# First-batch keys less their maximum on TensorE, float32 attention products for two batches, and a replanned order

## The chip, the core and the metric

The kernel runs on one core of one Trainium2 chip. The metric is the device time of one execution in microseconds (us), as the median of several runs. An order of instructions is written out by a planner in the kernel itself, so an edit of one operation, or of one of the planner's prices, may move any other instruction on its engine.

## The reference, cut to what matters

Linear attention over four batches of eight heads (576 rows of 64), then two feed-forward layers over all 2304 rows:

```python
q_s = exp(q - max(q, axis=-1)); q_s = q_s / (sum(q_s, axis=-1) + 1e-9)
k_s = exp(k - max(k, axis=2));  k_s = k_s / (sum(k_s, axis=2) + 1e-9)
kv  = einsum('bhsd,bhse->bhde', k_s, v)
x   = einsum('bhsd,bhde->bhse', q_s, kv)   # then [2304, 512]
h = x @ w_in1;  x2 = (h * sigmoid(1.702 * h)) @ w_out1
h = x2 @ w_in2; out = (h * tanh(softplus(h))) @ w_out2
```

Shapes: w_in is 512 x 2048, w_out 2048 x 512, everything float32.

## The kernel before

Rows go in six blocks of 384 (NB). A batch of 576 rows is one and a half blocks, so blocks 1 and 4 straddle two batches. Per block, `attention(blk)` makes the transposed input `xt` of the first layer: a high part rounded to float32r and the low part that is left (`hi_lo`: ACT copies, DVE subtracts). Every large product is the sum of three float32r products, high by high, high by low and low by high (`SPLIT`).

A *unit* is one batch and one pair of heads (four units to a batch). `k_load` and `v_load` fetch it: k as one DMA whose rows are 1536 B long in both memories, v as two DMAs of 256 B pieces, because the tile `vt` leaves two columns of ones after each 64 columns (they give the sum of the exponentials). `k_max` forms the maximum of k over the rows: a strided `reduce_max` on DVE over six chunks (L444), a transpose on TensorE (L454), a second `reduce_max` (L456), and a transpose that spreads the result over partitions (L461). `k_kv` copies that to SBUF on ACT (L468), subtracts it from k on DVE or GpSimd (through the helper `either`, L321), exponentiates on ACT (L471), multiplies with v in float32 on TensorE (L477, twelve products, two records each), and divides by the sum: ACT writes the high part of `kv` (L498), DVE the low part (L505). The first batch has a PSUM bank (`acc`) for each unit; later ones share the bank `at[0]`.

For q, `q_soft` takes the softmax, `q_turn` transposes (L578) and splits the result into high and low (`hi_lo`, L565 on ACT and L570 on DVE, tile named g in the trace because `qT` is a part of g2), and `x_part` multiplies with `kv` in three float32r products (L596) and splits again into `xt`.

`weight` brings a 512 KB chunk of a weight matrix and reforms it: two scalings on ACT (L338), three DVE steps (L377, L384, L389), a high part copied by ACT (L329) and a low part subtracted on DVE (L321). Each layer has 32 chunks. The first layer's 12 matmuls for one of its 16 columns of h are `gemm_in` (L666), followed by `gelu` (L679, L684), `gelu_split` (L329, L321) and 12 matmuls of `gemm_out` (L707). The second layer is L666 into `hp` and L838. These matmuls are called the spine here.

`Plan` holds all of these operations with their engines, costs and dependences. `best()` places them by urgency, forward and backward, six times, and keeps the order whose modelled end is earliest. `either`, `copy` and `scaled` leave the engine to it. Before the first spine matmul it fills TensorE's gaps with transposes of the identity (`idle`, L873) and models the clock by the columns that went through (`clocked`). `attention(t + 1)` is handed in while block t runs; attention(0) comes first of all. All DMAs are issued on SP's queue in the planned order. Of the DVE and GpSimd operations some are marked as a pair that may not overlap (`from_pair`).

Of the kernel before, what the change touches and what calls it, by code (L numbers as in the profile page):

```python
# [19 lines left out]
class Plan:  # L20
# [18 lines left out]

    def op(self, ways, reads, writes):  # L40


        i = len(self.ops)
        before = {self.last_write.get(key) for key in [*reads, *writes]}
        for key in writes:
            before.update(self.readers.get(key, ()))
        for key in reads:
            self.readers.setdefault(key, []).append(i)
        for key in writes:
            self.last_write[key] = i  # L50
            self.readers[key] = []
        self.ops.append((ways, sorted(before - {None, i})))
# [22 lines left out]
    def order(self, links, urgency, ways=None):  # L75
# [33 lines left out]

        def clocked(t, begin, cost):  # L110
# [23 lines left out]
        while any(queues.values()):  # L134
# [16 lines left out]
            if e == PE and not ways:  # L151
                idle, cost = clocked(f, begin, cost)
                started = started or i == self.first
# [56 lines left out]
def tile_attention_moe_moe(  # L210
# [35 lines left out]
    NLATE = 3  # L246
    NRAW = 4
    ND = 3
    SPLIT = ((0, 0), (0, 1), (1, 0))
# [4 lines left out]

    ident = const.tile([P, P], F32, name="ident")
    W = [const.tile([P, 2, 1024], F32R, name=f"W{i}") for i in range(NFC - NLATE)]
    xt = [const.tile([P, NCC, 2, NB], F32R, name=f"xt{i}") for i in range(2)]
# [20 lines left out]
    kv = [ap.tile([P, 2, P], F32R, name=f"kv{i}") for i in range(NHP)]  # L278
    pmt = [ap.tile([KP, P], F32, name=f"pmt{i}") for i in range(NHP)]
    mcol = ap.tile([P, NHP], F32, name="mcol")  # L280
    rs = ap.tile([P, NHP], F32, name="rs")
    qs = ap.tile([P, 2, 12], F32, name="qs")
# [4 lines left out]
    kt += [sp.tile([KP, 2, KC, D], F32, name=f"kt{i}") for i in range(2, NHP)]  # L287
    vt += [sp.tile([KP, 2, KC, D + 2], F32, name=f"vt{i}") for i in range(1, NHP)]
    qr = [sp.tile([P, 4, NCT, D], F32, name=f"qr{i}") for i in range(2)]

    nc.scalar.preload_act_table_set("exp_and_others")
    make_identity(nc, ident)
    for t in vt:
        nc.gpsimd.memset(t[:, :, :, D : D + 2], 1.0)
# [11 lines left out]

    def pe(ns, reads, writes, fn):
        plan.op([(PE, ns, fn, False)], reads, writes)
# [41 lines left out]
    for i in range(NHP):  # L350
        plan.op([(POOL, 350.0, lambda i=i: nc.gpsimd.memset(f32(kv[i]), 0.0), False)], [], [("kv", i)])


# [70 lines left out]
    def v_load(u):  # L424
        b, hp = divmod(u, NHP)
        key = ("vt", v_tile(u))
        for j in range(2):
            dma(
# [7 lines left out]

    def k_max(u, ps1, ps2, key1, key2):
        kk = ("kt", k_tile(u))
        m = mcol[:, u % NHP : u % NHP + 1]
        dve(  # L440
            1310,
            [kk],
            [("pm", u % NHP)],
            lambda: nc.vector.reduce_max(  # L444
                out=pmt[u % NHP].rearrange("p (j d) -> p j d", j=2),
                in_=kt[k_tile(u)].rearrange("p j c d -> p j d c"),
                axis=AX.X,
            ),
        )
        pe(  # L450
            110,
            [("pm", u % NHP)],
            [key1],
            lambda: nc.tensor.transpose(ps1[:, 0:KP], pmt[u % NHP], ident[0:KP, 0:KP]),  # L454
        )
        dve(96, [key1], [("mc", u % NHP)], lambda: nc.vector.reduce_max(out=m, in_=ps1[:, 0:KP], axis=AX.X))  # L456
        pe(
            110,
            [("mc", u % NHP)],
            [key2],  # L460
            lambda: nc.tensor.transpose(ps2[0:KP, :], m.to_broadcast([P, KP]), ident),  # L461
        )

    def k_kv(u, ps2, ps3, key2, key3):
        kk = ("kt", k_tile(u))
        t, bc = kt[k_tile(u)], pmt[u % NHP]
        pk = ("pm", u % NHP)
        act(128, [key2], [pk], lambda: nc.scalar.activation(out=bc, in_=ps2[0:KP, :], func=AF.Copy), psum=True)  # L468
        m = bc.rearrange("p (j o d) -> p j o d", j=2, o=1).to_broadcast([KP, 2, KC, D])
        either(768, ALU.subtract, lambda: t, lambda: t, lambda: m, [kk, pk], [kk])  # L470
        act(768, [kk], [kk], lambda: nc.scalar.activation(out=t, in_=t, func=AF.Exp))  # L471

# [11 lines left out]

        pe(1375, [kk] + [("vt", v_tile(u), j) for j in range(2)], [key3], mm)

        o = kv[u % NHP]
        r = rs[:, u % NHP : u % NHP + 1]
        rk = ("rs", u % NHP)
        dve(1, [key3], [rk], lambda: nc.vector.tensor_scalar_add(r, ps3[:, D : D + 1], 1e-9))  # L490
        dve(1, [rk], [rk], lambda: nc.vector.reciprocal(r, r))
        for j in range(2):
            s = slice(j * D, (j + 1) * D)
            act(
                140,
                [key3, rk, ("kv", u % NHP)],
                [("kv", u % NHP, 0, j)],
                lambda s=s: nc.scalar.activation(out=o[s, 0, s], in_=ps3[s, 0:D], func=AF.Copy, scale=r[s, :]),  # L498
                psum=True,
            )  # L500
            dve(
                120,
                [key3, rk, ("kv", u % NHP, 0, j)],
                [("kv", u % NHP, 1, j)],
                lambda s=s: nc.vector.scalar_tensor_tensor(  # L505
                    out=o[s, 1, s],
                    in0=ps3[s, 0:D],
                    scalar=r[s, :],
                    in1=f32(o[s, 0, s]),
                    op0=ALU.mult,  # L510
                    op1=ALU.subtract,
                ),
            )
# [59 lines left out]
    def q_turn(blk, hp, ps, key):  # L573
        keys = [("qt", j, d) for j in (2 * (hp % 2), 2 * (hp % 2) + 1) for d in (0, 192)]

        def turn():
# [7 lines left out]
        pe(330, keys, [key], turn)  # L584
        t = qT[hp % 2]
        hi_lo(
            NB, lambda: t[:, 0, :], lambda: t[:, 1, :], lambda: ps[:, 0:NB], [key], ("qT", hp % 2, 0), ("qT", hp % 2, 1)
# [5 lines left out]
    def x_part(blk, hp, ps, key, r):  # L593
        def mm():
            for n, (a, b) in enumerate(SPLIT):
# [6 lines left out]
                )  # L602

        kvk = [("kv", hp, a, j) for a in range(2) for j in range(2)]
        n = NB if r is None else NB // 2
        i = 0 if r is None else r[0] // 64
        pe(521 if r is None else 340, kvk + [("qT", hp % 2, 0), ("qT", hp % 2, 1)], [key], mm)
        x = xt[blk % 2]
# [13 lines left out]
    def attention(blk):  # L622
# [3 lines left out]
        b = last[0]  # L626
        if blk == 0:
            kps = lambda hp: [(acc[hp][:, i * P : (i + 1) * P], ("acc", hp)) for i in range(3)]
        else:
            kps = lambda hp: [(at[0][:, i * P : (i + 1) * P], ("at", 0)) for i in range(3)]  # L630
        xps = lambda i: (at[1], ("at", 1)) if fresh and blk else (at[i % 2], ("at", i % 2))
        us = [b * NHP + hp for hp in range(NHP)] if fresh else []

        def unit(hp):
            u = us[hp]
            p = kps(hp)
            k_load(u)
            v_load(u)
            k_max(u, p[0][0], p[1][0], p[0][1], p[1][1])
            k_kv(u, p[1][0], p[2][0], p[1][1], p[2][1])  # L640

# [141 lines left out]
    def hb_keys(n):  # L783
        return [("h", 0), ("h", 1)] if (n + 1) % 2 == 0 else [("at", 0), ("at", 1)]

# [86 lines left out]
    def idle():  # L872
# [9 lines left out]
        + [("kt", i) for i in range(2, NHP)]  # L882
        + [("vt", i, j) for i in range(1, NHP) for j in range(2)]
        + [("qr", i) for i in range(2)],
    )
# [8 lines left out]
    for n in range(NS):  # L894
# [14 lines left out]
        if n == NS - NFC:  # L909
# [6 lines left out]
                + [("qt", j, d) for j in range(4) for d in (0, 192)]  # L916
                + [("kv", hp, a, j) for hp in range(NHP) for a in range(2) for j in range(2)]
                + [("pm", i) for i in range(NHP)]
                + [(s, i) for s in ("mc", "rs") for i in range(NHP)]
# [56 lines left out]
```

## Time and profile before

| what | us |
|---|---|
| median of 3 runs | 912.94 (912.01 to 913.74) |
| profiled execution, its own time | 910.09 |
| span of the profiled execution | 908.3 |
| TensorE matmul busy | 879.6 |
| VectorE (DVE) busy | 418.0 |
| ScalarE (ACT) busy | 364.1 |

The busy shares are means over stages with different limits, so the stages have to be read one by one: the slices of the page tell where an engine is full, the table by stretches tells how full, and the waits tell who was late there. "PE" is TensorE's matmul row, "PEld" its weight loads. Matmul ends are modelled and overlap, so the distance from the start of one group to the start of the next is a better measure of their rate than the busy time.

### The profile page before, as it was taken

How to read it: one execution, taken by the hardware profiler on the slowest of the kernel's cores; microseconds unless marked ns; L12 is line 12 of the kernel's file. 1: busy time of each engine (PE TensorE's matmuls, PEld its weight loads, DVE VectorE, ACT ScalarE, POOL GpSimd, SP SyncE). 2: the span in 40 equal slices, each digit the busy share in tenths (PEclk: the TensorE clock that was granted, in tenths of full speed). 3: DMA queues.
4: the chain of work that ended last, by engine and by line, in shares of the span. 5: the costliest groups of instructions: out<-in, count | busy, mean ns of one | idle time of the engine just before them, and what ended most of it. 6: DMA issues, size and time to landing. Idle time of an engine off the chain costs nothing.

```text
span 908.3 us, 12391 instructions
## 1 busy us (share of the span) xinstructions
PE 879.6 (97%) x5030; PEld 822.6 (91%) x5030; DVE 418.0 (46%) x758; ACT 364.1 (40%) x654; POOL 8.6 (1%) x18
## 2 busy tenths in 40 slices
PE   8897889999999999999999999999999999999998
PEld 7775669999998999999999999899999998998997
DVE  8999999255368247424899941110111011111100
ACT  4787674233245235323678841222222212212221
POOL 0001000000000000000000000000000000000000
PEclk9999999999999999999999999999999999999999
DMA  9665655002023112200245501001001001000000
GB/s 251 157 204 164 185 153 172 24 18 88 1 70 85 57 44 57 79 1 10 70 140 186 173 13 70 35 1 70 35 1 70 35 1 70 35 1 1 35 1 35
DMA packets 66616, 65.80 MB, mean 72 GB/s; under 512 B 37120, under 2 KB 57600, under 8 KB 66048
## 3 DMA queue, kind: packets, MB, share of 16 engines
q1 hardware_dynamic: 66560, 65.03, 23.7%
q8 instruction: 39, 0.64, 0.3%
q14 instruction: 17, 0.14, 0.1%
HBM read 54.00 MB, written 11.01 MB: 72 GB/s over the span
## 4 chain that ended last, share of the span: by engine, by line
PE 82%; DVE 8%; DMA 5%; ACT 2%; SPq 2%; issue 1%; DVEq 0%; ACTq 0%
PE hp L666 22%; PE acc L838 22%; PE acc L707 18%; PE h L666 17%; DMA raw<-in_moe_w_out_dram 2%; DMA raw<-in_moe_w_in_dram 2%; SPq L312 2%; PE at L477 1%; DVE dec L384 1%; DVE dec L389 1%; DVE pmt L444 1%; PE at L596 1%; DVE W L321 1%; PE at L578 1%; DMA qt<-in_q_dram 1%
## 5 line engine op out<-in xcount | busy, mean ns | idle before, releaser
L666 PE MATMUL h<-xt,W 128*128 128x384 f32 x1152 | 226.5, 340 | 9.7 <-DVE gt L684 4.8
L707 PE MATMUL acc<-g,W 128*128 128x384 f32 x1152 | 222.0, 338 | 1.8 <-DVE W L321 1.6
L666 PEld LDWEIGHTS h<-xt,W 128*128 128x128 f32 x1152 | 201.1, 189 | 16.4 <-DVE W L321 4.6
L666 PE MATMUL hp<-xt,W 128*128 128x384 f32 x1152 | 208.4, 335 | 0.0
L838 PE MATMUL acc<-W,g 128*128 128x512 f32 x864 | 206.1, 392 | 0.0
L666 PEld LDWEIGHTS hp<-xt,W 128*128 128x128 f32 x1152 | 201.9, 188 | 3.7
L707 PEld LDWEIGHTS acc<-g,W 128*128 128x128 f32 x1152 | 200.0, 188 | 4.1 <-DVE W L321 2.7
L838 PEld LDWEIGHTS acc<-W,g 128*128 128x128 f32 x864 | 161.6, 188 | 32.7
L321 DVE TENSOR_TENSOR g<-gt,g 128x384 fp32r<-128x384 f32 (+1 forms) x110 | 67.2, 611 | 173.1 <-ACT g L329 173.0
L321 DVE TENSOR_TENSOR g<-tb,g 128x768 fp32r<-128x768 f32 x32 | 30.6, 957 | 210.8 <-ACT g L329 210.8
L815 ACT ACTIVATE tb<-hp 128x768 f32<-128x768 f32 x32 | 26.0, 813 | 177.1 <-PE hp L666 177.1
L329 ACT ACTIVATE g<-gt 128x384 fp32r<-128x384 f32 (+1 forms) x112 | 63.7, 569 | 73.9 <-PE acc L707 68.3
L679 ACT ACTIVATE gt<-h 128x384 f32<-128x384 f32 x96 | 46.7, 488 | 89.5 <-PE h L666 89.1
L684 DVE SCALAR_TENSOR_TENSOR gt<-gt,h 128x384 f32<-128x384 f32 x96 | 52.6, 548 | 60.7 <-ACT gt L679 60.5
L815 ACT ACTIVATE gt<-hp 128x768 f32<-128x768 f32 x16 | 13.0, 812 | 96.3 <-PE hp L666 96.3
L338 ACT ACTIVATE dec<-raw 128x512 f32<-128x512 f32 x63 | 42.3, 675 | 18.5 <-DVE W L321 9.6
L338 ACT ACTIVATE raw<-raw 128x512 int32<-128x512 uint32 x63 | 42.5, 677 | 9.0 <-DMA raw<-in_moe_w_in_dram 5.1
L384 DVE SCALAR_TENSOR_TENSOR dec<-raw,dec 128x512 int32<-128x512 int32 x64 | 44.4, 694 | 0.3
L321 DVE TENSOR_TENSOR W<-dec,W 128x512 fp32r<-128x512 f32 x64 | 43.6, 681 | 0.6
L389 DVE CUSTOM_DVE_ANT_0 dec<-raw,dec 128x1024 uint16<-128x1024 uint16 x64 | 43.5, 683 | 0.2
L329 ACT ACTIVATE W<-dec 128x512 fp32r<-128x512 f32 x64 | 40.2, 629 | 8.0 <-DVE dec L389 8.0
L377 DVE TENSOR_SCALAR dec<-dec 128x512 int32<-128x512 int32 x64 | 27.7, 433 | 1.9 <-ACT dec L338 1.8
(65 smaller groups left out, 414.9 us busy)
## 6 DMA issues: line engine op xcount, KB each, us to landing
raw<-in_moe_w_in_dram SPq DMA_DIRECT2D x32, 512.0 KB, 3.8
raw<-in_moe_w_out_dram SPq DMA_DIRECT2D x32, 512.0 KB, 3.7
x2d<-xt SPq DMA_DIRECT2D x16, 384.0 KB, 3.2
xt<-x2d SPq DMA_DIRECT2D x4, 1536.0 KB, 6.3
kt<-in_k_dram SPq DMA_DIRECT2D x16, 288.0 KB, 4.5
vt<-in_v_dram SPq DMA_DIRECT2D x32, 144.0 KB, 3.7
out_dram<-dec SPq DMA_DIRECT2D x18, 256.0 KB, 2.1
qt<-in_q_dram SPq DMA_DIRECT2D x24, 96.0 KB, 2.8
```

The costliest lines, as they stand in the source:

```text
L321: return lambda: engine.tensor_tensor(out=out(), in0=in0(), in1=in1(), op=op)
L329: (ACT, act_ns(n), lambda: nc.scalar.activation(out=out(), in_=in_(), func=AF.Copy), False),
L338: (ACT, act_ns(512), lambda: nc.scalar.activation(out=out, in_=in_, func=AF.Copy, scale=scale), False),
L377: lambda: nc.vector.tensor_single_scalar(out=a, in_=a, scalar=3, op=ALU.logical_shift_left),
L384: lambda: nc.vector.scalar_tensor_tensor(out=a, in0=hi_w, scalar=-0x80000000, in1=a, op0=ALU.bitwise_and, op1=ALU.bitwise_or),
L389: dve(512, [rl], [da], lambda: nc.vector.tensor_tensor(out=a, in0=a, in1=lo_w, op=ALU.add), pair=True)
L666: nc.tensor.matmul(out=h(), lhsT=w_mm(fc, 0, a, cc), rhs=xt[buf][:, cc, b, :], start=cc == 0 and i == 0, stop=cc == NCC - 1 and i == 2,)
L679: act(NB, [hk, ("tables",)], [tk], lambda: nc.scalar.activation(out=t, in_=h, func=AF.Tanh, scale=0.851), psum=True)
L684: lambda: nc.vector.scalar_tensor_tensor(out=t, in0=t, scalar=1.0, in1=h, op0=ALU.add, op1=ALU.mult),
L707: nc.tensor.matmul(out=acc[dm][:, 0:NB], lhsT=w_mm(fc, 1, a, dm), rhs=g[n % 2][:, b, :], start=fc == 0 and i == 0, stop=fc == NFC - 1 and ...
L815: nc.scalar.activation(out=tb[i], in_=hb(n), func=AF.Mish)
L838: nc.tensor.matmul(out=acc[bank], lhsT=g2[gi][:, j, a, c * P : (c + 1) * P], rhs=w_mm(2 * pr + j, 1, b, 0, 512), start=pr == 0 and j == 0 ...
```

## The change

- In the first batch the maximum is no longer subtracted by DVE. After the transposed maximum is in `mcol`, TensorE forms k minus the maximum in PSUM by two float32 products for each head (identity by k, plus the spread maximum by a negative identity `minus`), and ACT takes the exponential straight from PSUM, one head at a time (`k_first`). Units share two `acc` banks each, so units 0 and 2 use the same two, and units 1 and 3.
- In later batches the spread maximum is subtracted by DVE out of PSUM, without the copy to SBUF and without the choice of GpSimd (`k_later`).
- The strided `reduce_max` over six chunks becomes three elementwise maxima (384, 128 and 128 elements a partition).
- For batches 0 and 1 (blocks 0 to 2 of q), q and `kv` stay float32: one copy each, no low part, and `x_part` is one float32 product.
- v of the first batch is loaded densely (four DMAs with 1536 B rows) into `vr` or a part of gt, and copied to `vt` by ACT or GpSimd. Two `vr` buffers and gt serve four units, so the fourth load waits for the first copy.
- In the planner, DMAs cost by 280 instead of 360 bytes per ns, float32 products count as quarter columns in the clock's model, and `from_pair` leaves TensorE out.
- `hb_keys` is written otherwise with the same result, and the DMA scratch is smaller.

The core of the diff, with long calls drawn together:

```diff
-            return max(t, held[POOL if e == DVE else DVE]) if pair else t
+            return max(t, held[POOL if e == DVE else DVE]) if pair and e != PE else t
...
-            t, rate = begin, 2.4 / slow(begin)
+            t, rate = begin, (0.6 if whole else 2.4) / slow(begin)
...
-            [(DMA, max(size * slow / 360.0, 650.0), lambda: nc.sync.dma_start(out=out(), in_=in_()), False)],
+            [(DMA, max(size * slow / 280.0, 650.0), lambda: nc.sync.dma_start(out=out(), in_=in_()), False)],
...
+        if b == 0:
+            dense, dk = vr[hp % 3], [("vr", hp % 3)] if hp % 3 < 2 else [("gt", 0), ("gt", 1)]
+            dma(S * 512, [], dk, lambda: dense,
+                lambda: v[b, 2 * hp : 2 * hp + 2].rearrange("h (p c) d -> p h (c d)", c=KC))
+            to = vt[v_tile(u)][:, :, :, 0:D]
+            of = dense.rearrange("p j (c d) -> p j c d", d=D)
+            plan.op([
+                    (ACT, act_ns(768), lambda: nc.scalar.activation(out=to, in_=of, func=AF.Copy), False),
+                    (POOL, 1200.0, lambda: nc.gpsimd.tensor_copy(out=to, in_=of), True),
+                ], dk, [key + (j,) for j in range(2)])
+            return
...
+        largest = lambda n, out, in0, in1, reads, writes: dve(
+            n, reads, writes, lambda: nc.vector.tensor_tensor(out=out, in0=in0, in1=in1, op=ALU.max), pair=True)
+        largest(384, x, t[:, :, 0:3], t[:, :, 3:6], [kk], [xk])
+        largest(128, wide, x[:, :, 0], x[:, :, 1], [xk], [pk])
+        largest(128, wide, wide, x[:, :, 2], [xk, pk], [pk])
+        pe(110, [pk], [key], lambda: nc.tensor.transpose(ps, pm, ident[0:KP, 0:KP]))
+        dve(96, [key], [mk], lambda: nc.vector.reduce_max(out=m, in_=ps, axis=AX.X))
...
+    def k_first(u, ps, keys):
+        k_max(u, ps[0][:, NB : NB + KP], keys[0])
+        for j in range(2):
+            def less(j=j):
+                o = ps[j][0:KP, 0:NB]
+                nc.tensor.matmul(out=o, lhsT=ident[0:KP, 0:KP],
+                    rhs=t[:, j].rearrange("p c d -> p (c d)"), start=True, stop=False)
+                nc.tensor.matmul(out=o.rearrange("p (c d) -> p c d", d=D), lhsT=m.to_broadcast([P, KP]),
+                    rhs=minus[:, j * D : (j + 1) * D].rearrange("p (o d) -> p o d", o=1).to_broadcast([P, KC, D]),
+                    start=False, stop=True)
+            pe(1330, [("kt", k_tile(u)), ("kt", k_tile(u), j), mk], [keys[j]], less, whole=True)
+            act(NB, [keys[j]], [("kt", k_tile(u), j)],
+                lambda j=j: nc.scalar.activation(
+                    out=t[:, j].rearrange("p c d -> p (c d)"), in_=ps[j][0:KP, 0:NB], func=AF.Exp), psum=True)
...
+    def k_later(u, ps1, ps2, key):
+        k_max(u, ps1[:, 0:KP], key)
+        pe(110, [mk], [key], lambda: nc.tensor.transpose(ps2[0:KP, :], m.to_broadcast([P, KP]), ident))
+        far = ps2[0:KP, :].rearrange("p (j o d) -> p j o d", j=2, o=1).to_broadcast([KP, 2, KC, D])
+        dve(768, [kk, key], [kk], lambda: nc.vector.tensor_tensor(out=t, in0=t, in1=far, op=ALU.subtract))
+        act(768, [kk], [kk], lambda: nc.scalar.activation(out=t, in_=t, func=AF.Exp))
...
+        whole = u < WHOLE * NHP
+            o = kv32[u % NHP][s, s] if whole else kv[u % NHP][s, 0, s]
...
+            if whole:
+                continue
...
+        if blk * NB < WHOLE * S:
+            o = qT32[hp % 2]
+            plan.op([
+                    (ACT, act_ns(NB, True), lambda: nc.scalar.activation(out=o, in_=ps[:, 0:NB], func=AF.Copy), False),
+                    (DVE, dve_ns(NB), lambda: nc.vector.tensor_copy(out=o, in_=ps[:, 0:NB]), False),
+                ], [key], [("qT32", hp % 2)])
+            return
...
+            pe(665 if r is None else 340, [("kv32", hp, j) for j in range(2)] + [("qT32", hp % 2)], [key], mm_whole, whole=True)
...
+                banks = [acc[2 * (hp % 2) + i] for i in range(2)]
```

## Rows read from the trace of the kernel before

**Rows 1.** The page: DVE's busy tenths in 40 slices of the span.

```profile
DVE  8999999255368247424899941110111011111100
```

**Rows 2.** Busy time by stretches; each row: stretch, its length, busy time of engines, clock, DMA.

```profile
core 0: us, PE busy (x) PEld busy (x) DVE busy (x) ACT busy (x) POOL busy (x), PEclk, DMA share, GB/s
...
45.00:50.00 5.00, 4.51 (x24) 3.87 (x24) 5.00 (x11) 4.47 (x8) 0.00 (x0) 1.00 0.63 203
...
80.00:90.00 10.00, 5.46 (x26) 4.33 (x26) 10.00 (x18) 6.64 (x12) 2.86 (x2) 1.00 0.48 147
...
140.00:150.00 10.00, 10.00 (x59) 10.00 (x59) 10.00 (x18) 6.45 (x14) 0.00 (x0) 1.00 0.58 212
```

**Rows 3.** TensorE timeline: start, length, engine, line, operation, shapes, count.

```profile
30.29 1.30 PE L666 MATMUL h<-xt,W 128*128 128x384 f32 x6
...
50.56 2.25 PE L707 MATMUL acc<-g,W 128*128 128x384 f32 x12
...
55.76 2.24 PE L707 MATMUL acc<-g,W 128*128 128x384 f32 x12
...
137.74 2.25 PE L707 MATMUL acc<-g,W 128*128 128x384 f32 x12
139.83 2.27 PE L666 MATMUL h<-xt,W 128*128 128x384 f32 x12
```

**Rows 4.** TensorE's waits from 28 to 150 us: total us, times, longest.

```profile
PE h L666 <- DVE gt L684: 4.8, 3, 2.3
PE at L477 <- ACT kt L471: 4.5, 3, 2.3
```

**Rows 5.** Groups by line and form, 0 to 150 us: busy us, mean ns, idle before.

```profile
L444 DVE TENSOR_REDUCE pmt<-kt 96x128 f32<-96x768 f32 x10 | 15.0, 1502 | 4.4 <-DMA kt<-in_k_dram 4.4
...
L321 DVE TENSOR_TENSOR kt<-kt,pmt 96x768 f32<-96x768 f32 x8 | 7.5, 943 | 0.0
L471 ACT ACTIVATE kt<-kt 96x768 f32<-96x768 f32 x8 | 6.7, 835 | 3.5 <-DVE kt L321 3.5
...
L477 PE MATMUL acc<-vt,kt 96*64 96x66 f32 x96 | 5.8, 225 | 1.1 <-ACT kt L471 1.1
...
L570 DVE TENSOR_TENSOR g<-at,g 128x384 fp32r<-128x384 f32 x8 | 4.3, 545 | 0.8 <-ACT g L565 0.8
...
L570 DVE TENSOR_TENSOR xt<-at,xt 128x192 fp32r<-128x192 f32 x8 | 2.7, 334 | 0.0
...
L505 DVE SCALAR_TENSOR_TENSOR kv<-at,rs,kv 64x64 fp32r<-64x64 f32 x8 | 2.3, 284 | 1.0 <-ACT kv L498 0.9
```

**Rows 6.** DVE timeline, the first two instructions and the last gap of the start.

```profile
4.01 1.47 DVE L444 TENSOR_REDUCE pmt<-kt 96x128 f32<-96x768 f32 x1 [4.01 <-DMA kt<-in_k_dram]
5.39 0.94 DVE L551 TENSOR_REDUCE qs<-qr 128x12 f32<-128x768 f32 x1
...
24.41 0.58 DVE L505 SCALAR_TENSOR_TENSOR kv<-acc,rs,kv 64x64 fp32r<-64x64 f32 x2 [1.71 <-issue]
```

**Rows 7.** SP timeline: DMA issues of k and v at the start.

```profile
1.67 1.49 SPq L312 DMA_DIRECT2D kt<-in_k_dram  x3
...
3.70 5.48 SPq L312 DMA_DIRECT2D vt<-in_v_dram  x4
```

**Rows 8.** GpSimd and DVE timelines where both are busy.

```profile
79.64 1.79 POOL L321 TENSOR_TENSOR qt<-qt,qs 128x768 f32<-128x768 f32 x1 [77.18 <-DVE qs L551]
...
120.15 1.41 POOL L321 TENSOR_TENSOR g<-gt,g 128x384 fp32r<-128x384 f32 x1 [13.46 <-ACT g L329]
...
80.48 1.50 DVE L384 SCALAR_TENSOR_TENSOR dec<-raw,dec 128x512 int32<-128x512 int32 x1
...
119.88 1.56 DVE L444 TENSOR_REDUCE pmt<-kt 96x128 f32<-96x768 f32 x1
```

**Rows 9.** A stretch at a lower clock (columns as in rows 2), and TensorE in it.

```profile
92.00:94.00 2.00, 2.00 (x8) 2.00 (x7) 1.56 (x4) 1.01 (x2) 0.00 (x0) 0.50 0.35 80
...
92.03 3.62 PE L666 MATMUL h<-xt,W 128*128 128x384 f32 x12
```

More of the change, by code (lines that the diff above doesn't have):

```diff
@@ L108, in ends, with clocked @@
             return from_pair(i, w, max(free.get(e, 0.0), queues[e][i][0])) + ahead + cost + spare.get(e, 0.0)
-        def clocked(t, begin, cost):
+        def clocked(t, begin, cost, whole):
             def slow(t):
@@ L151, in order @@
             if e == PE and not ways:
-                idle, cost = clocked(f, begin, cost)
+                idle, cost = clocked(f, begin, cost, self.ops[i][0][w][3])
                 started = started or i == self.first
@@ L247, in tile_attention_moe_moe @@
     NRAW = 4
+    WHOLE = 2
     ND = 3
@@ L279, in tile_attention_moe_moe @@
     pmt = [ap.tile([KP, P], F32, name=f"pmt{i}") for i in range(NHP)]
+    kv32 = [ap.tile([P, P], F32, name=f"kv32_{i}") for i in range(NHP)]
+    qT32 = [ap.tile([P, NB], F32, name=f"qT32_{i}") for i in range(2)]
     mcol = ap.tile([P, NHP], F32, name="mcol")
+    kx = [ap.tile([KP, 2, 3, D], F32, name=f"kx{i}") for i in range(2)]
     rs = ap.tile([P, NHP], F32, name="rs")
@@ L288, in tile_attention_moe_moe @@
     vt += [sp.tile([KP, 2, KC, D + 2], F32, name=f"vt{i}") for i in range(1, NHP)]
+    vr = [sp.tile([KP, 2, KC * D], F32, name=f"vr{i}") for i in range(2)] + [gt2[0:KP]]
     qr = [sp.tile([P, 4, NCT, D], F32, name=f"qr{i}") for i in range(2)]
@@ L305, in dve, with pe @@
         plan.op([(DVE, dve_ns(n, fast), fn, pair or fast)], reads, writes)
-    def pe(ns, reads, writes, fn):
-        plan.op([(PE, ns, fn, False)], reads, writes)
+    def pe(ns, reads, writes, fn, whole=False):
+        plan.op([(PE, ns, fn, whole)], reads, writes)
     def dma(size, reads, writes, out, in_, slow=1):
         plan.op(
-            [(DMA, max(size * slow / 360.0, 650.0), lambda: nc.sync.dma_start(out=out(), in_=in_()), False)],
+            [(DMA, max(size * slow / 280.0, 650.0), lambda: nc.sync.dma_start(out=out(), in_=in_()), False)],
             reads,
@@ L426, in v_load @@
         key = ("vt", v_tile(u))
+        if b == 0:
+            dense, dk = vr[hp % 3], [("vr", hp % 3)] if hp % 3 < 2 else [("gt", 0), ("gt", 1)]
+            dma(
+                S * 512,
+                [],
+                dk,
+                lambda: dense,
+                lambda: v[b, 2 * hp : 2 * hp + 2].rearrange("h (p c) d -> p h (c d)", c=KC),
+            )
+            to = vt[v_tile(u)][:, :, :, 0:D]
+            of = dense.rearrange("p j (c d) -> p j c d", d=D)
+            plan.op(
+                [
+                    (ACT, act_ns(768), lambda: nc.scalar.activation(out=to, in_=of, func=AF.Copy), False),
+                    (POOL, 1200.0, lambda: nc.gpsimd.tensor_copy(out=to, in_=of), True),
+                ],
+                dk,
+                [key + (j,) for j in range(2)],
+            )
+            return
         for j in range(2):
@@ L435, in v_load, with k_max @@
             )
-    def k_max(u, ps1, ps2, key1, key2):
+    def k_max(u, ps, key):
         kk = ("kt", k_tile(u))
[L439 to L448, printed above, removed]
-        )
[L450 to L462, printed above, removed]
@@ L464, in k_kv @@
-    def k_kv(u, ps2, ps3, key2, key3):
-        kk = ("kt", k_tile(u))
[L466 to L471, printed above, removed]
+        t, m, mk = kt[k_tile(u)], mcol[:, u % NHP : u % NHP + 1], ("mc", u % NHP)
@@ new lines, in k_max @@
+        pm, pk = pmt[u % NHP], ("pm", u % NHP)
+        wide = pm.rearrange("p (j d) -> p j d", j=2)
+        x = kx[u % 2]
+        xk = ("kx", u % 2)
+        largest = lambda n, out, in0, in1, reads, writes: dve(
+            n, reads, writes, lambda: nc.vector.tensor_tensor(out=out, in0=in0, in1=in1, op=ALU.max), pair=True
+        )
+        largest(384, x, t[:, :, 0:3], t[:, :, 3:6], [kk], [xk])
+        largest(128, wide, x[:, :, 0], x[:, :, 1], [xk], [pk])
+        largest(128, wide, wide, x[:, :, 2], [xk, pk], [pk])
@@ L473, in mm, with k_kv @@
+    def k_kv(u, ps3, key3):
+        kk = ("kt", k_tile(u))
+        t = kt[k_tile(u)]
         def mm():
@@ L483, in mm @@
                     )
-        pe(1375, [kk] + [("vt", v_tile(u), j) for j in range(2)], [key3], mm)
-        o = kv[u % NHP]
+        pe(1375, [kk] + [("kt", k_tile(u), j) for j in range(2)] + [("vt", v_tile(u), j) for j in range(2)], [key3], mm, whole=True)
         r = rs[:, u % NHP : u % NHP + 1]
@@ L602, in mm, with mm_whole @@
                 )
+        def mm_whole():
+            nc.tensor.matmul(
+                out=part(ps[:, 0:NB], r),
+                lhsT=kv32[hp],
+                rhs=part(qT32[hp % 2], r),
+                start=True,
+                stop=True,
+            )
         kvk = [("kv", hp, a, j) for a in range(2) for j in range(2)]
@@ L635, in unit @@
             u = us[hp]
-            p = kps(hp)
             k_load(u)
             v_load(u)
-            k_max(u, p[0][0], p[1][0], p[0][1], p[1][1])
-            k_kv(u, p[1][0], p[2][0], p[1][1], p[2][1])
+            if blk == 0:
+                banks = [acc[2 * (hp % 2) + i] for i in range(2)]
+                keys = [("acc", 2 * (hp % 2) + i) for i in range(2)]
+                k_first(u, banks, keys)
+                k_kv(u, banks[0][:, NB : NB + P], keys[0])
+            else:
+                p = [at[0][:, i * P : (i + 1) * P] for i in range(3)]
+                k_later(u, p[0], p[1], ("at", 0))
+                k_kv(u, p[2], ("at", 0))
         parts = [(0, 64), (64, 128)] if straddle else [None]
@@ L883, in tile_attention_moe_moe @@
         + [("vt", i, j) for i in range(1, NHP) for j in range(2)]
+        + [("vr", i) for i in range(2)]
         + [("qr", i) for i in range(2)],
@@ L917, in tile_attention_moe_moe @@
                 + [("kv", hp, a, j) for hp in range(NHP) for a in range(2) for j in range(2)]
+                + [("kv32", hp, j) for hp in range(NHP) for j in range(2)]
+                + [(s, i) for s in ("qT32", "kx") for i in range(2)]
                 + [("pm", i) for i in range(NHP)]
```

55 lines of the change are left out of this document (42 added, 13 removed).

## Prediction

> **What bounds the kernel now.** I read the slices first, then the table by stretches, then TensorE's waits, then the groups by form.
>
> The slices show two kernels in one. DVE is at 9 or more in the first six slices and falls away after that [rows 1]; a slice is 22.7 us, so DVE is full until some 140 us. The stretches say what that does to TensorE: at 45 to 50 us DVE is busy 5.00 of 5.00 us and TensorE 4.51, at 80 to 90 DVE 10.00 of 10.00 and TensorE 5.46; at 140 to 150 both are at 10.00 [rows 2]. From there TensorE runs twelve matmuls in 139.83 - 137.74 = 2.09 us [rows 3] and only its own work can shorten the run. Before it, the pair of twelves that costs 2 x 2.09 = 4.18 us takes 55.76 - 50.56 = 5.20 us [rows 3]: 1.0 us lost in each period, and far more while the second batch's attention is put in between. The waits confirm the owner: the largest wait of TensorE after 28 us is for DVE's gelu product, three times 4.8 us together, and the next, 4.5 us, for exponentials that themselves wait for DVE's subtraction [rows 4, 5].
>
> So the rule for this case: work taken from DVE before about 136 us moves the time at which TensorE becomes full, and with it the end, nearly one for one; work taken from it later is worth nothing, and work given to TensorE later is paid in full. The cover is large enough: the spine begins at 30.29 us [rows 3], and one block costs 32 twelves, 67 us, of the 106 us to 136 us; with 5.8 us for batch 1's L477 [rows 5] and, as an estimate, as much again for the other attention products, TensorE still has over 20 us of gaps to give back.
>
> **Part by part: DVE.** Means come from the groups by form [rows 5], eight units (batches 0 and 1) and eight pairs of heads (blocks 0 and 1) being ahead of the point where TensorE is full.
>
> - Maxima. A strided reduce takes 1.50 us. No elementwise maximum stands in the trace. The nearest rows are two-operand instructions: 384 elements 0.545 us, 192 elements 0.334. That is 1.1 ns an element, so 128 elements come to 0.264, and three instructions to 0.545 + 2 x 0.264 = 1.07. The other end: each of the two dependent instructions also waits for the one ahead, at most the 0.08 us by which neighbours overlap otherwise, so 1.07 to 1.23 us. I take 1.07, as the planner can put other work in between. Gain 0.43 a unit, 8 units: 3.4 us (2.2 to 3.4).
> - First batch's subtraction: 0.943 us, four units: 3.8 us. In batch 1 it stays on DVE and reads PSUM. The 384-element subtraction that reads PSUM (0.545) lies on the line through the SBUF one of 768 (0.943), so nothing is gained or lost there.
> - Low part of `kv`: two instructions of 0.284 a unit, eight units: 4.5 us. (The row shows eight of them; the first batch has eight more like it.)
> - Low part of q: 0.545, eight pairs: 4.4 us, if ACT makes the one copy; zero if the planner gives the copy to DVE.
>
> Sum by means 16.1 us. Means overlap their neighbours: the second instruction starts 1.38 us after one of 1.47 [rows 6], so each counts 0.08 too much. Net, 4 + 16 + 8 instructions go and 16 come, 12 x 0.08 = 1.0. **15.1 us** leave DVE's queue, 9 of them from the start, 6 from batch 1.
>
> **Part by part: the rest.** TensorE's new products of the first batch: 24 records of 66 columns take about 1.44 us on end, that is twelve products at 0.12 us or 1.8 ns a column; four products of 384 columns a unit are 2.8 us, 11 us for four units. They lie in the start, where TensorE fills gaps with identity transposes; their cover is that filling, and their cost is nothing unless the chain of one unit decides the start. The float32 `x_part` costs 384 x 1.8 = 0.69 us against three at 2.09/12 [rows 3], 0.52; for block 2, whose attention comes in the full stretch, 4 x 0.17 = 0.7 us are paid. In blocks 0 and 1 TensorE has gaps.
>
> ACT: four dense copies of v, 768 elements, 0.84 us each by the exponential of that size [rows 5], and each exponential in two halves, against eight copies of the spread maximum that go. At 80 to 90 us ACT has 3.4 us of 10 free [rows 2], in the start more: nothing by itself.
>
> SP and DMA: four issues of v take 5.48 us of SP, three of k 1.49 [rows 7]. Eight v issues become four like those of k: 10 us of SP become 2, and the weights queued behind them are issued earlier. The fourth v load waits for the copy of the first, and the weights behind it wait too; what they feed is the reforming on DVE, which has a queue of its own at that time. I count nothing: DVE has work from 4.01 us on, with gaps of 1.71 us and less after its first instruction [rows 6]. In `k_later` DVE waits for the transpose of the maximum where ACT waited before, and holds what is behind it on DVE for up to one transpose and a semaphore; as the planner places it, nothing to 0.3 us four times.
>
> Against the 15.1 us I set: 0.7 for block 2; 1 to 3 us of new gaps on DVE in the start, because 9 us less work there meets the same arrival of k and v (it had 1.71 us of gaps of its own); up to 1 us for the waits on dependent instructions. 15.1 - 0.7 - 2 - 0.5 = **12 us**. Bounds: 15.1 plus the old gaps and a better start would be 19; with all costs at their upper ends 9.
>
> **A row and a rule on GpSimd.** While GpSimd multiplied for 1.79 us from 79.64, DVE's two-operand L384 at 80.48 took 1.50 us, 0.8 more than its neighbours; while GpSimd subtracted from 120.15, the reduce L444 at 119.88 took 1.56, as usual [rows 8]. The Trainium skill, "SBUF — State Buffer", section "Who interferes with whom", states this as a rule: a DVE instruction with two SBUF inputs and a GpSimd instruction that reads SBUF exclude each other for the whole instruction, and a reduce never contends. By that rule, the change swaps an instruction that is immune for three that are not; the trace agrees in these two places.
>
> **The rivals.**
>
> *The start does not shorten.* The units now share PSUM banks in pairs, so unit 2's maximum waits until unit 0's `kv` is out: the chain of a unit is three maxima, transpose, reduce, 2.8 us of products, exponential, 1.44 us of products, copies, about 8 us, and two of them in a row from 4.01 us plus v's arrival end near 24 us, as late as the old one with 24.41 [rows 6]. Then only batch 1's 6 us count, less 0.7: gain 5.3, profile 904.8. For it: the chains; against it: the old start went on to 35 us because DVE had reforming and splitting left, and that does get less.
>
> *The plan takes it back.* The planner may put the four v copies on GpSimd and the eight q copies on DVE. Price: 4 x 0.8 us of held DVE [rows 8] and 8 x 0.47 = 3.8: 7.0 of the 12 gone, gain 5, profile 905; with a poorer order by 2 us more, 907. For it: the copies have both ways; against it: DVE is full, and the planner models that.
>
> *Slower: the clock.* At 92 to 94 us the granted clock was 0.50, the 1.2 GHz level, behind the stretch in which TensorE was busy for 5.46 of 10 us [rows 2]; twelve matmuls took 3.62 us [rows 9] instead of 2.09. The change puts more float32 products and fewer float32r ones around the early spine. If the low level holds through periods of 5.2 us in which TensorE needs 2 x 4.18 = 8.4 us, each costs 3.2 us: four such periods (21 us) eat the gain, seven make 10 us of loss, 920 in the profile, 923 in the median. For it: the gaps remain; against it: the clock was 1.00 at 45 to 50 and at 80 to 90 us, gaps and all [rows 2], and fewer gaps are to come.
>
> *It does nothing:* the reordering elsewhere eats what DVE gains; 910.
>
> **How the numbers follow.** Forecast 0.58, the start 0.18, the plan 0.12, the clock 0.09, nothing 0.03. The profile's own execution took 910.09 us, 2.85 below the median of the runs shown, 912.94; a gain is the same for both. So the likeliest time is 912.94 - 12 = 900.9; its own range is 912.94 - 19 to - 9, 894 to 904. The start gives 907.6, the plan 908 to 910, the clock 923. The range of 8 in 10 reaches from 893 to 910.5. About 0.2% (1.8 us) is what a measurement of this kernel can tell from none: faster means below 911.1. Forecast, start and most of the plan are faster: 0.86; same 0.05; slower 0.09.
>
> **What would show it.** Right: the first L666 some 5 to 9 us earlier than 30.29; DVE's total busy time down by some 22 us (16.1, and in the covered part eight maxima of batches 2 and 3 and four low parts of block 2); the stretch in which TensorE reaches 10.00 of 10.00 beginning near 124 us instead of 136; twelves still at 2.09 us after it. Wrong: a first L666 near 30 us with DVE idle ahead of it (the start); GpSimd busy at 5 to 20 us with DVE instructions of 1.5 us beside it (the plan); a granted clock under 1.00 ahead of 80 us (the clock). If the start is shorter but the full stretch begins as late, the bound between was not DVE's amount of work but the order, and my rule of one for one fails.

## The result, and the profile after

The changed kernel took 899.77 us (median of 4 runs) beside 912.48 us for the kernel before: ratio 0.9868, 95% interval 0.9839 to 0.9898. Timed again in as many rounds as the experiments it gave 899.6 beside 909.5 us: ratio 0.9888, interval 0.9873 to 0.9903. The forecast of 900.9 us holds. The forecast gain of 12 us lies between the two measured ones, 12.7 and 9.9 us; the second rests on more runs of the kernel before. The way there was in part another one than forecast.

The profiled execution of the changed kernel took 898.94 us with a span of 897.2, 11.1 us less than the span before. Its table by stretches (columns as in rows 2; PEclk stands ahead of the DMA share):

```profile
20.00:25.00 5.00, 4.47 (x30) 3.78 (x30) 4.70 (x14) 4.12 (x9) 0.00 (x0) 0.50 1.00 248
...
40.00:45.00 5.00, 2.07 (x22) 2.07 (x23) 5.00 (x11) 4.46 (x11) 0.00 (x0) 0.50 0.81 233
45.00:50.00 5.00, 4.38 (x16) 2.90 (x15) 5.00 (x14) 4.82 (x11) 0.00 (x0) 0.70 0.80 221
...
80.00:90.00 10.00, 10.00 (x60) 9.96 (x59) 10.00 (x22) 6.90 (x14) 0.00 (x0) 1.00 0.47 151
...
140.00:150.00 10.00, 10.00 (x59) 10.00 (x58) 3.04 (x6) 3.59 (x8) 0.00 (x0) 1.00 0.50 160
```

At 80 to 90 us TensorE now is busy 10.00 of 10.00 us where it was 5.46 [rows 2]; ahead of 50 us it is idler than before, and twice at the lower clock. TensorE's timeline shows the same from inside (start, length, line, count, and in brackets what it waited for):

```profile
19.38 2.52 PE L533 MATMUL acc<-vt,kt 96*64 96x66 f32 x24 [5.48 <-ACT kt L510]
...
42.93 2.52 PE L533 MATMUL acc<-vt,kt 96*64 96x66 f32 x24 [3.97 <-ACT kt L510]
...
46.26 1.74 PE L751 MATMUL h<-xt,W 128*128 128x384 f32 x3
...
56.21 2.35 PE L751 MATMUL h<-xt,W 128*128 128x384 f32 x12 [2.94 <-DVE gt L769]
58.39 2.24 PE L792 MATMUL acc<-g,W 128*128 128x384 f32 x12
60.47 2.24 PE L751 MATMUL h<-xt,W 128*128 128x384 f32 x12
```

The spine begins at 46.26 us, 16 us later than before [rows 3]. But from 56.21 us its twelves follow at 58.39 - 56.21 = 2.2 and then 2.08 us, through the whole attention of the second batch, with one more wait of 0.3 us. The periods of 5.2 us are gone. TensorE's waits from 18 to 150 us answer rows 4:

```profile
PE acc L533 <- ACT kt L510: 10.7, 3, 5.5
PE h L751 <- DVE gt L769: 2.9, 1, 2.9
PE at L638 <- DVE xt L630: 2.3, 2, 1.1
```

The 4.8 us for DVE's gelu product are now 2.9, and the 4.5 us for exponentials of the second batch are gone; instead TensorE waits 10.7 us in the start, for exponentials of the first batch. Two lines of TensorE's timeline and four of ACT's show what held them:

```profile
11.72 0.81 PE L497 MATMUL acc<-minus,mcol 128*96 128x384 f32 x2
...
34.44 0.81 PE L497 MATMUL acc<-minus,mcol 128*96 128x384 f32 x2
```

```profile
17.59 0.85 ACT L450 ACTIVATE vt<-vr 96x768 f32<-96x768 f32 x1
18.34 0.61 ACT L337 ACTIVATE W<-dec 128x512 fp32r<-128x512 f32 x1
18.86 0.47 ACT L510 ACTIVATE kt<-acc 96x384 f32<-96x384 f32 x1
...
42.41 0.47 ACT L510 ACTIVATE kt<-acc 96x384 f32<-96x384 f32 x1
```

k less its maximum was ready in PSUM by 12.5 and 35.3 us, and its exponential ran at 18.86 and 42.41 us: in between ACT, in the planned order, mostly scaled and copied weights and copied v. DVE did not become idle there: 0 to 60 us, it is busy for 54.38 us (53.37 before). It reformed weights. The last of the first layer's 32 chunks shows it; DVE's timeline, first of the kernel before and then of the changed one:

```profile
141.08 0.68 DVE L321 TENSOR_TENSOR W<-dec,W 128x512 fp32r<-128x512 f32 x1
```

```profile
123.74 0.68 DVE L329 TENSOR_TENSOR W<-dec,W 128x512 fp32r<-128x512 f32 x1
```

It ends at 141.76 before and at 124.42 after, 17.3 us earlier. The first low part is written at 18.50 instead of 29.65 us. So the planner now starts on the weights early and on the spine late: the first low part is written 27.8 us ahead of the spine's first matmul (18.50 against 46.26 us), where it was 0.6 us before.

The groups by form, 0 to 140 us, for the operations that the prediction had to guess (busy us, mean ns):

```profile
L476 DVE TENSOR_TENSOR kx<-kt 96x384 f32<-96x384 f32 x10 | 5.4, 542 | 4.0 <-DMA kt<-in_k_dram 4.0
...
L476 DVE TENSOR_TENSOR pmt<-kx 96x128 f32<-96x128 f32 x10 | 2.8, 280 | 0.1
L476 DVE TENSOR_TENSOR pmt<-pmt,kx 96x128 f32<-96x128 f32 x10 | 2.8, 280 | 0.0
...
L522 DVE TENSOR_TENSOR kt<-kt,at 96x768 f32<-96x768 f32 x4 | 3.8, 948 | 0.3 <-PE at L520 0.3
...
L450 ACT ACTIVATE vt<-vr 96x768 f32<-96x768 f32 x3 | 2.5, 848 | 0.6 <-DMA vr<-in_v_dram 0.4
...
L650 ACT ACTIVATE qT<-at 128x384 f32<-128x384 f32 x8 | 3.7, 476 | 0.0
```

Three maxima take 0.542 + 0.280 + 0.280 = 1.10 us (forecast 1.07), the subtraction out of PSUM 0.948 (0.943 assumed). All v copies and all q copies went to ACT. GpSimd did nothing after its setup.

### The profile page after: what moved, and what is told of

Its sections match the earlier page's. It is cut to its first block, busy times and chain, and to the rows that moved or that the text cites. A ratio compares the mean times of both kernels' runs of the same rounds, so it can differ in the third digit from the quotient of the medians.

```text
span 897.2 us, 12178 instructions
## 1 busy us (share of the span) xinstructions
PE 873.7 (97%) x4933; PEld 818.1 (91%) x4933; DVE 399.0 (44%) x765; ACT 361.2 (40%) x643; POOL 3.0 (0%) x19
## 4 chain that ended last, share of the span: by engine, by line
PE 89%; DVE 6%; DMA 2%; ACT 1%; issue 1%; DVEq 0%; ACTq 0%
PE hp L751 22%; PE acc L923 22%; PE acc L792 21%; PE h L751 20%; PE at L533 2%; DMA raw<-in_moe_w_out_dram 1%; DVE dec L398 1%; DVE dec L393 1%; PE at L667 1%; DVE W L329 1%; PE at L638 1%; PE at L676 1%; DMA raw<-in_moe_w_in_dram 1%; DVE dec L386 0%; DVE gt L769 0%
## 5 line engine op out<-in xcount | busy, mean ns | idle before, releaser
L751 PE MATMUL h<-xt,W 128*128 128x384 f32 x1152 | 223.6, 339 | 2.9 <-DVE gt L769 2.9
L792 PE MATMUL acc<-g,W 128*128 128x384 f32 x1152 | 219.7, 337 | 0.0
L337 ACT ACTIVATE g<-tb 128x768 fp32r<-128x768 f32 x32 | 27.1, 846 | 0.9
```

What stands on the lines that cost most here:

```text
L337: (ACT, act_ns(n), lambda: nc.scalar.activation(out=out(), in_=in_(), func=AF.Copy), False),
L751: nc.tensor.matmul(out=h(), lhsT=w_mm(fc, 0, a, cc), rhs=xt[buf][:, cc, b, :], start=cc == 0 and i == 0, stop=cc == NCC - 1 and i == 2,)
L792: nc.tensor.matmul(out=acc[dm][:, 0:NB], lhsT=w_mm(fc, 1, a, dm), rhs=g[n % 2][:, b, :], start=fc == 0 and i == 0, stop=fc == NFC - 1 and ...
```

## Experiments

Two theories. **A**: what counts is DVE's amount of work up to the last weight chunk, as the prediction had it. **B**: the gain comes from the start or from the new order and prices. A later form, **C**, gives it to the dense loads of v.

Five kernels keep the order of the instructions as planned and have work in addition that nobody reads. Six undo a part of the change or do one part alone, and are planned anew. One is the changed kernel again.

### Work put in, order kept

```diff
+    for n in range(12, 24):            # behind the 13th to 24th chunk
+        plan.behind["W", n] = [three reduce_max of ident (128 elements) into scr]
```

> The kernel before, its order kept, with three small reduces on DVE (128 elements into a scratch column, about 0.2 us each from start to start) behind each of the 13th to 24th weight chunks: some 7 us of DVE work that nobody reads. Theory A (the amount of DVE work up to the last chunk sets the end): 6 to 8 us slower than the kernel before. Theory B (the length of the start sets it, and work placed behind the start is hidden): 0 to 2 us slower.

Measured: 921.08 us, ratio 1.0124 (1.0111 to 1.0137): 11.3 us slower, beyond A's 6 to 8. The estimate of the work put in, some 7 us, was low. In DVE's timeline a group of three holds the queue from 64.97 to 65.80:

```profile
64.97 0.92 DVE L959 TENSOR_REDUCE scr<-ident 128x1 f32<-128x128 f32 x3
65.80 0.68 DVE L397 CUSTOM_DVE_ANT_0 dec<-raw,dec 128x1024 uint16<-128x1024 uint16 x1
```

Twelve times 0.83 are 10.0 us in, 10.8 us out of the span (919.1 against 908.3): A, about one for one.

```diff
+    plan.ahead["in", 24] = [54 transposes of ident into at[0]]   # the 7th group of gemm_in
```

> The kernel before, its order kept, with 54 idle transposes (0.11 us each, 6.0 us in all) on TensorE ahead of its 7th group of the first layer. Theory A: TensorE has gaps of 1 us in each period and more later, which take them up: 0 to 1 us slower. Theory B, that whatever delays TensorE in its early part delays the end: 6 us slower.

Measured: 913.23 us, ratio 1.0045 (1.0032 to 1.0057), 3.4 us slower by the medians and 3.1 by the spans; neither 0 to 1 nor 6. A line of TensorE's timeline and one of DVE's tell why:

```profile
58.22 6.06 PE L957 MATMUL at<-ident 128*128 128x128 f32 x54
```

```profile
67.44 0.69 DVE L329 TENSOR_TENSOR W<-dec,W 128x512 fp32r<-128x512 f32 x1 [3.30 <-ACT W L337]
```

TensorE's 6 us were mostly taken up by its gaps. But ACT waited for the h that came late, a copy of W stood behind that on ACT, and DVE waited for this copy: 3.30 us. That is close to what came out at the end.

The same two edits were made to the changed kernel.

> The changed kernel, its order kept, with the same three small reduces on DVE behind each of the 13th to 24th weight chunks, some 7 us. These chunks are ready up to 25 us before TensorE needs them, but the last two only 2 to 5 us. Theory A (DVE's amount still counts, less the slack of the last chunks): 3 to 6 us slower than the changed kernel, that is 7 to 10 us faster than the kernel before. Theory B (from 56 us TensorE is full, and DVE is out of the picture): 0 to 1 us slower than the changed kernel, 12 us faster than before.

Measured: 911.33 us, ratio 1.0012 (1.0001 to 1.0024), against 0.9888 for the changed kernel: 11.3 us slower for the 10.0 us put in. Both forecasts are missed, B's by more. TensorE's timeline shows where the time went:

```profile
57.58 2.95 PE L760 MATMUL h<-xt,W 128*128 128x384 f32 x12 [2.75 <-DVE gt L779]
...
63.87 2.24 PE L760 MATMUL h<-xt,W 128*128 128x384 f32 x12
...
93.35 1.32 PE L760 MATMUL h<-xt,W 128*128 128x384 f32 x6
99.69 0.45 PE L529 MATMUL at<-ident,mcol 128*96 128x128 f32 x1 [5.03 <-DVE mcol L491]
...
101.86 3.01 PE L802 MATMUL acc<-g,W 128*128 128x384 f32 x12
104.71 0.49 PE L647 MATMUL at<-ident,qt 128*128 128x128 f32 x3
```

In the changed kernel the same operations stand at 56.21, 60.47, 89.62, 91.25, 92.45 and 94.53 us. So TensorE was 1.4 us late at the first of them, 3.4 at the second, 3.7 at the third, and 10.2 behind the wait of 5.03 us. It was not the weights, which were ahead: the maximum of the second batch's first unit stands in the same queue on DVE, and TensorE's later instructions stood behind it. The rest is in part a lower granted clock: 0.76 over 57 to 64 us and 0.54 over 98 to 104 us, where the changed kernel had 1.00 from 50 us on. B's "DVE is out of the picture" is out for a kept order. But that 11.3 us come out for 10.0 is a sum of waits and low clock; it does not show one for one.

> The changed kernel, its order kept, with the same 54 transposes (6.0 us) ahead of the 7th group of the first layer, at about 64 us, where TensorE has no gap any more. Theories A and B alike: 5 to 6 us slower than the changed kernel, some 7 us faster than the kernel before. If it is under 3 us, TensorE is not full after 56 us as its timeline says.

Measured: 905.28 us, ratio 0.9949 (0.9937 to 0.9961), against 0.9888: 5.5 us for 6.0, as expected (the transposes stand at 73.74 us and not at 64). In the changed kernel TensorE has nothing to give any more. DVE then waited 5.03 us for the gelu of the late h, and the weights behind that in its queue came late too.

### One part undone, planned anew

```diff
-    WHOLE = 2
+    WHOLE = 0
```

> The changed kernel with q and kv of batches 0 and 1 split into high and low parts again (three float32r products); planned anew. It gives back to DVE 16 low parts of kv and 12 of q (8 ahead of the point where its work thins out): 16 x 0.20 + 8 x 0.47 = 7.0 us by starts. Theory A (each us of DVE ahead of that point is a us of the end): 6 to 7 us slower than the changed kernel, ratio to the kernel before about 0.994. Theory B (the gain comes from the new order and prices, not from the work on DVE): within 2 us of the changed kernel, ratio about 0.987.

Measured: 899.94 us, ratio 0.9887 (0.9866 to 0.9907): the same as the changed kernel (0.9888). A's number is missed, B's is met.

```diff
-        largest(384, x, t[:, :, 0:3], t[:, :, 3:6], [kk], [xk])
...
+        dve(1310, [kk], [pk], lambda: nc.vector.reduce_max(out=wide, in_=t.rearrange("p j c d -> p j d c"), axis=AX.X))
```

> The changed kernel with the strided reduce in place of the three elementwise maxima; planned anew. By starts a reduce holds DVE for 1.42 us and the three maxima for 0.47 + 0.20 + 0.20 = 0.87: eight units, 4.4 us. Theory A: 3 to 4.5 us slower than the changed kernel, ratio about 0.991. Theory B: within 2 us of it, ratio about 0.987.

Measured: 898.44 us, ratio 0.9875 (0.9854 to 0.9896): the same. A's number is missed again.

```diff
-                k_first(u, banks, keys)
+                k_later(u, banks[0][:, 0:P], banks[1][:, 0:P], keys[0], keys[1])
```

> The changed kernel with the first batch's k less its maximum formed on DVE again (out of PSUM, as in later batches) instead of on TensorE; planned anew. DVE gets 4 x 0.87 = 3.5 us more, and TensorE loses four float32 products a unit in the start, 11 us at full clock. Theory A: 3 to 4 us slower than the changed kernel, ratio about 0.991. Theory B, in the form that the start's length counts: the shorter chains on TensorE make it 2 us or more faster than the changed kernel, ratio 0.985 or less.

Measured: 900.7 us, ratio 0.9892 (0.9876 to 0.9909): the same within the intervals; A's number and B's are both missed. The first spine group came at 24.98 us, 21 us earlier than in the changed kernel, and that gained nothing.

```diff
# the kernel before, with
-            [(DMA, max(size * slow / 360.0, 650.0), ...
+            [(DMA, max(size * slow / 280.0, 650.0), ...
# and the two other prices of the change
```

> The kernel before with nothing but the planner's new prices (DMAs by 280 bytes per ns, float32 products as quarter columns, the pair rule without TensorE); planned anew, the same work on every engine. Theory A: DVE has the same amount to do, so within 2 us of the kernel before, ratio 0.998 to 1.002. Theory B: 5 us or more of the 12 come from the prices, ratio 0.994 or less.

Measured: 909.06 us, ratio 0.9988 (0.9975 to 1.0001): the prices alone are worth 1 us, if anything. B as an effect of the prices is out.

By now each of DVE's three reliefs could be left out singly and the gain stayed, and the prices alone did not make it. Either the one part that had not been undone makes it (C), or the parts together do more than is used (A with some to spare). The last runs separate these.

```diff
-        if b == 0:
+        if b < 0:      # in v_load
```

> The changed kernel with v of the first batch loaded as before (eight DMAs of 256 B pieces straight into vt, no copy on ACT); planned anew. Theory A (DVE's amount, with several us to spare in the changed kernel, so that one part given back is absorbed by a new order; the loads are hidden): within 2 us of the changed kernel, ratio to the kernel before 0.986 to 0.989. Theory C (the dense loads free SP and let the reforming of weights start 11 us earlier, and that is the gain): 6 us or more slower than the changed kernel, ratio 0.994 or more.

Measured: 899.95 us, ratio 0.9897 (0.9882 to 0.9912): the same. C is out.

The three reliefs of DVE undone in one kernel:

```diff
-    WHOLE = 2
+    WHOLE = 0
...
-        largest(384, x, t[:, :, 0:3], t[:, :, 3:6], [kk], [xk])
+        dve(1310, [kk], [pk], lambda: nc.vector.reduce_max(out=wide, in_=t.rearrange("p j c d -> p j d c"), axis=AX.X))
...
-                k_first(u, banks, keys)
+                k_later(u, banks[0][:, 0:P], banks[1][:, 0:P], keys[0], keys[1])
```

> The changed kernel with all three reliefs of DVE undone together (split q and kv, strided reduce, first batch's subtraction on DVE), the dense loads of v, the new prices and the subtraction out of PSUM kept; planned anew. DVE gets 7.0 + 4.4 + 3.5 = 14.9 us back. Theory A: what one part alone did not show appears when all three are gone, 8 us or more slower than the changed kernel, ratio to the kernel before 0.996 to 1.0. Theory C (the dense loads make the gain): ratio 0.991 or less.

Measured: 907.29 us, ratio 0.9975 (0.9963 to 0.9986), 7.9 us slower than the changed kernel, at the edge of A's "8 us or more" and with its ratio; C's ratio is excluded. What is left of the change then, dense loads, prices and the subtraction out of PSUM, is worth 2.2 us together.

### The start's clock

```diff
+    plan.ahead["kvmm", 1] = [fill(48)]; plan.ahead["kvmm", 2] = [fill(10)]; plan.ahead["kvmm", 3] = [fill(36)]
+    plan.ahead["turn", 2] = [fill(10)]; plan.ahead["turn", 3] = [fill(10)]
```

> The changed kernel, its order kept, with idle transposes put into TensorE's gaps of the start (48, 10 and 36 ahead of the second to fourth unit's product with v, 10 ahead of each of the last two transposes of q), so that the granted clock does not fall to 0.50 at 20 to 25 and 40 to 45 us. Theory A with TensorE full from 56 us on: the first spine group comes some 2 us earlier than 46 us and the end with it, 1 to 3 us faster than the changed kernel; if DVE alone sets the end under this order, 0.

Measured: 898.51 us, ratio 0.9879 (0.9866 to 0.9893), against 0.9888: not told apart. The same stretch as above, with the gaps filled:

```profile
20.00:25.00 5.00, 4.74 (x53) 4.27 (x51) 5.00 (x14) 4.78 (x10) 0.00 (x0) 1.00 0.99 268
```

The granted clock is 1.00 instead of 0.50, the spine begins at 44.74 instead of 46.26 us, and the span is 0.7 us shorter. So the low clock of the start costs about a microsecond at most, and these runs do not tell that from nothing.

> The changed kernel as it is, timed beside the kernel before in as many rounds as the experiments: ratio 0.986 to 0.989, which sets the line that the others are compared with.

Measured: 899.6 us, ratio 0.9888 (0.9873 to 0.9903). This is the line for the comparisons above.

### One table for all of them

The end of the last weight chunk's low part on DVE (from DVE's timeline: start and length of the last), the span, and the difference, in us. GpSimd made two of the 32 low parts in `split_back` and one in `reduce_back`, none of them the last.

| kernel | last chunk ends | span | span less last chunk |
|---|---|---|---|
| before | 141.8 | 908.3 | 766.5 |
| dve_more_before | 152.0 | 919.1 | 767.1 |
| pe_more_before | 145.3 | 911.4 | 766.1 |
| prices_only | 140.3 | 907.2 | 766.9 |
| dve_back | 139.3 | 905.5 | 766.2 |
| split_back | 131.6 | 897.8 | 766.2 |
| reduce_back | 127.6 | 896.7 | 769.1 |
| sub_back | 128.7 | 899.2 | 770.6 |
| changed | 124.4 | 897.2 | 772.8 |
| after_again | 124.9 | 897.5 | 772.6 |
| warm | 123.8 | 896.5 | 772.7 |
| v_back | 122.9 | 898.0 | 775.1 |
| dve_more_after | 134.5 | 908.4 | 773.9 |
| pe_more_after | 130.5 | 903.2 | 772.7 |

Six kernels whose last chunks differ by 20 us end 766.1 to 767.1 us after it: there the weight stream, and so DVE, sets the end (in `pe_more_before` the stream was itself held up by the late h). No kernel comes under 766. In the changed kernel 6.3 us more lie between, and TensorE, full from 56.21 us, sets the end. This explains the single parts: `split_back` gave work back to DVE, its last chunk came 7.1 us later, the 6.3 us went to nothing, and the end stayed. (That 7.1 is so near its forecast of 7.0 us is in part chance, since GpSimd took two low parts of weights over.) From `dve_back` to the changed kernel the last chunk moves by 139.3 - 124.4 = 14.9 us; of these the end shows 8.3 us in the spans.

Two rows show the limits of this reading. The 6.3 us are slack of the last chunk, not of all that stands in DVE's queue: `dve_more_after`, with its order kept, ends 11.2 us later. And in `pe_more_after` the difference stays at 772.7 although it was TensorE that was delayed, because the last chunk came 6.1 us later with it. So the difference alone does not name the engine; whether TensorE is full ahead of the last chunk has to be read beside it.

## Why the prediction held, point by point

- *DVE's first 140 us bound the kernel.* Shown for the kernel before: a microsecond put in or held up there came out at the end in two ways (10.0 and 10.8, 3.30 and 3.1 by the spans), and `dve_back` takes most of the gain away. The slices were misread, though: they show 8 and then six nines, which end at 159 us, not at 136. What ends near 140 us is TensorE's waiting and the first layer's weights (141.76); DVE's work goes on.
- *15.1 us leave DVE's queue ahead of that point.* Right in size: 14.9 us by the last chunks of `dve_back` and the changed kernel. The terms differ more than the sum. (The overlap of neighbours read off [rows 6] is 1.47 - 1.38 = 0.09 and not 0.08, worth 0.1 us.) By the starts that the experiments went by, the maxima give 4.4 us where 3.4 was forecast, and the low parts of q 3.8 where 4.4 was. The low parts of `kv` were put at 0.20 us each in the experiments, 3.2 us; but a pair of them holds DVE for 0.51 us (24.41 [rows 6] to the next start at 24.92), so 16 of them are 4.1, and the three parts come to 15.8 us instead of the 14.9 expected for `dve_back`. There GpSimd took four low parts of gelu in turn, 0.55 us each on DVE. That both figures read 14.9 is chance.
- *DVE's total busy time falls by some 22 us.* 418.0 to 399.0, 19.0; GpSimd had done two operations of q and two of gelu before (0.95 and 0.55 us each on DVE) that DVE does now, 3.0 us.
- *One for one to the end.* Wrong as put. It holds until TensorE is full; from there 6.3 us of the relief lie unused. The forecast had TensorE's gaps as cover ("over 20 us") and did not ask from what moment on there would be none: the planner spent much of the cover on a later start of the spine.
- *2 us of new gaps on DVE in the start.* Wrong: DVE was as busy there as before, since the planner filled it with weights. The terms that did differ from the sum: 2.5 us more came from the loads, the prices and the subtraction out of PSUM (141.8 to 139.3 us for the last chunk; 1.5 of them in `prices_only`), which I had counted as nothing, and 6.3 us were not used. 17.3 - 6.3 is the 11.1 us of the spans, with rounding. That it lies so near the 12 of the sum is luck in these terms, not in the 15.1.
- *First L666 5 to 9 us earlier; full stretch from 124 us.* Wrong by more than the signs: 16 us later, and full from 56 us. The order decides when the spine starts; under a weight stream that sets the end, a late start without gaps and an early start with gaps can be worth the same. `sub_back`, with its start at 24.98 us, ends 2 us later in the span than the changed kernel.
- *The start as a rival.* A late start came, beyond the rival's size, but hardly by its mechanism. The shared banks show as one wait of 0.5 us (L481 for L556; 5.3 us in `v_back`); the 10.7 us are waits for exponentials that stood on ACT behind weights. It cost no gain that the runs show: `sub_back`, without it, is no faster, and DVE had weights to do meanwhile.
- *The plan as a rival.* Did not come: v and q copies went to ACT. The Trainium skill's rule in "SBUF — State Buffer", "Who interferes with whom", was hardly put to the test on the maxima, as GpSimd was idle beside them in the changed kernel. In `sub_back` one maximum, at 82.29 us, stands beside a GpSimd subtraction that began at 82.03: the maximum took its usual 0.28 us, and GpSimd's instruction 2.02 where one in `split_back` took 1.02.
- *The clock as a rival.* It did fall, to 0.50 at 20 to 25 and 40 to 45 us, where TensorE had waited and then ran float32 products. The mean granted clock of the profiled execution is 0.989 against 0.998. Twelve-matmul groups of the full stretch were not touched, and `warm` prices it at 1 us at most, not at 3.2 a period.
- *Float32 products.* Two float32 `x_part` products of block 0 take from 28.39 to 29.68 us on TensorE's timeline, 0.64 us each, against 0.69 forecast; block 2's, in the full stretch, were not priced by a run of their own.
- *The maxima.* The Trainium skill, "VectorE: DVE Perf Modes", section "The perf-mode tier table", gives a reduce and a float32 two-operand instruction the same rate. By that alone, as an estimate, 640 elements in three instructions against 768 in one would gain a sixth at most. The measured gain is 1.50 to 1.10 us, a quarter, and the measurement decides. A reduce of as many elements laid out in order (L551) takes 0.94 us [rows 6], less than the three maxima. It also differs in its groups (64 elements to one maximum instead of six), so whether the stride or the short groups make the reduce over chunks slow is not shown.

What stays open: why the planner's order starts the spine at 46 us in the changed kernel and whether an order exists that starts earlier and keeps it gapless. By the table such an order could end 124.4 + 766.5 = 890.9 us after the start, 6 us less; no run shows it. Filling TensorE's gaps in the start did not reach it, and no other attempt was made.

## What to carry to other kernels

Where one engine feeds a stream to another, measure from the end of the last item fed to the end of the kernel, over orders planned anew: while this number stays at its least, the feeder sets the time, and a microsecond there is a microsecond; when it grows, the fed engine does. Check it against the fed engine's own gaps, because with a kept order a delay of the fed engine can delay the feeder too and leave the number as it was. Undoing parts of a change one at a time can show nothing at all when the change gives more than is used; undo them together before calling them worthless. And a late start of the bound engine is no loss in itself: look for its last gap, not for its first instruction.

## What the runs showed of the hardware

A strided reduce over six chunks on DVE (96 x 768, float32, six elements to a maximum) takes 1.50 us, one of as many elements in order (128 x 768, 64 to a maximum) 0.94 us. Three small reduces of 128 elements that write the same column hold DVE for 0.83 us, 0.28 each and not the 0.2 that was expected. A float32 product of 384 columns, two records, was busy for 0.81 us at 11.72 us, where the granted clock was 1.00, and for 1.49 us at 25.21, where it was 0.50, the 1.2 GHz level.
